# A convolution of width 3 with batch norm and SiLU: the first stage's loads, weights and jobs in another order

## The chip, the core and the metric

The kernel runs on one core of a Trainium2 chip. The metric is the device time of one execution in microseconds; lower is better. Before the change, three executions took 180.88, 180.94 and 181.14 us, a median of 180.94 us.

## The reference

The input `x` has 2 batches of 2048 positions with 1024 channels, all in bf16. Three 1024 x 1024 matrices `w[k]` are applied to the positions before, at and after each output position, the products are added, and a batch norm and SiLU follow:

```
xp = jnp.pad(x, ((0, 0), (P, P), (0, 0)))
y = sum(jnp.einsum('bsc,cd->bsd', xp[:, k:k + S, :], w[k]) for k in range(K))
inv_std = 1.0 / jnp.sqrt(var + 1e-5)
y = (y - mean) * (g * inv_std) + b
return _silu(y)
```

## The kernel before, in words

The kernel computes six neighbouring outputs from eight transformed inputs, with eight products instead of eighteen. The 2048 positions of a batch are cut into 342 groups of six. One input **transform** turns eight neighbouring positions of each group into eight numbers; it is a matmul of a window of 128 positions (the weights, `xw`) with a constant matrix `rm` of 8 x 21 columns (L241). One window gives 21 groups; 16 windows (`NF`) give 336 of them, and a **short** block of 48 rows (`xl`, L255) gives the last 6.

**Tiles.** `x` is loaded as 16 tiles of 512 KB, one for each batch `bi` and block `ct` of 128 channels; a tile has 128 partitions (positions in the window) of 16 windows x 128 channels. I call them tile (bi, ct). Six buffers hold them (`XBUFS`). The weights come by output block `dc` (eight of 128 channels), 768 KB each, in the order w0, w2, w1 (`W0, W2, W1`); for dc 0 the first two arrive in one transfer and w1 in a second.

**Jobs.** A tile's 16 windows are three jobs of 6, 6 and 4 transforms. `Jobs.do` writes a job into two of the eight PSUM banks (`BANKS`: A is banks 4 and 5, B is 6 and 7, C is 2 and 3, D is 0 and 1), and DVE or ACT or both copy the banks to `T_sb` in SBUF (casts of L264 on ACT and L266 on DVE). In the order of the first stage, written out by hand in `ORDER`, a token such as `Bda` is a job in B, its first bank copied by DVE and the second by ACT; `Ad` is a job in A whose two banks DVE copies in one instruction; `s2d` is the short block in bank 2. These three kinds are all of the transform work.

**Weights.** The products at points 0 and 7 use w0 and w2 as they are. The six others use sums: `even` adds two arrays on POOL (L134, or on DVE with L140 in the later stages), `transform_w` adds or subtracts w1 or its double (L147), so that `u0`, `u1`, `u2` each have a plus and a minus half. `FirstWeights` gives the order for dc 0, `prepare_second` that for dc 1, `prepare_w` that for the rest.

**The first unit.** `First` is the product of (dc 0, batch 0), spread through the first stage so that PE has something to do between jobs (L414). In `ORDER` a plain number stands for that many matmuls of points 0 and 7 (`ends`, 16 in all, into banks 2 and 3), `p` and a number for matmuls of the other points (`todo`, 48 in all, into banks 1, 0 and 2). `m2a` doubles w1 on ACT. `+` takes one entry of `later`, a list of DVE operations that combine the products (`combine`, L309). `kept` holds the points 0 and 7 after they left their banks (`COPIES` says by which engine a product is copied).

**Later stages.** 14 `Unit`s follow, each for one (dc, bi), on alternating halves of PSUM, and two `Half`s for the last; each unit has eight products of eight matmuls of 342 columns (L294).

**Queues.** Every engine runs its instructions in the order in which the program gives them. SP issues nearly all loads; ACT issues `rm` and `prm` (four rows of batch-norm parameters). `scales()` computes the batch norm's factors on POOL (L220 to L225), ahead of the first weights.

Of the kernel before, what the change touches and what calls it, by code (L numbers as in the profile page):

```python
# [8 lines left out]
ALU = mybir.AluOpType  # L9
# [5 lines left out]
R = 6  # L15
# [1 line left out]
WT = 21  # L17
XBUFS = 6
LROWS = 48
SROW = 66  # L20
NTILES = 342
NBP = 384


# [2 lines left out]

BANKS = {"A": 4, "B": 6, "C": 2, "D": 0}
ORDER = (
    "Bad Aad Da Cda Bda Ad Da Bda s2d Aad Dad Bad 2 Aa Dda 1 Bda Aad 1 Dad 1 Bda 1 Aa 1 Dda 1 Bda 1 Ada "  # L30
    "Dda Bad 1 m2a 2 Dd 2 Bda Aad Dda 2 Bad Aad p4 Ca p1 Bad p2 Aad Cda Ba p1 Ada p2 Ca p1 Bda p2 Aad p1 "
    "Ca p1 Bda p1 Aa p1 Cd p2 Bad p5 + Cad Ba p4 s4a Ca Bda Aa"
)

W0, W2, W1 = range(3)
COPIES = {0: "a", 7: "d", 1: "d", 3: "d", 2: "a", 5: "a"}

@with_exitstack
def kernel(
# [2 lines left out]
    x: bass.AP,  # L42
    xl: bass.AP,
    w: bass.AP,
    prm_in: bass.AP,
    rm_in: bass.AP,
    out: bass.AP,
):
    nc = tc.nc
    B, CT, _, NF, _ = x.shape  # L50
    DC = w.shape[0]
    NB = NTILES
    LAST = NB - NF * WT
    NT = NF * WT
    H = P

# [19 lines left out]
    T_sb = [tpool.tile([P, CT, NJ, NB], BF16, name=f"T_sb{bi}") for bi in range(B)]  # L76


    rm = consts.tile([P, NJ, WT], BF16, name="rm")
    nc.scalar.dma_start(out=rm, in_=rm_in)  # L80
    prm = consts.tile([P, 4, DC], BF16, name="prm")


    zero = consts.tile([P, 1], FP32, name="zero")
    nc.gpsimd.memset(zero, 0.0)
    for n in (384, 384, 216):
        nc.tensor.matmul(
            ps[:, 3, 0:n], lhsT=zero.broadcast_to([P, P]), rhs=zero.broadcast_to([P, n]), start=True, stop=True,
        )
    zeros = consts.tile([P, 64], FP32, name="zeros")  # L90
    nc.vector.memset(zeros, 0.0)
    dummy = consts.tile([P, 2], FP32, name="dummy")
    nc.vector.memset(dummy, 0.0)

# [4 lines left out]
    nc.vector.memset(small, 0.0)  # L99

    def load_small(bi):
        nc.sync.dma_start(out=small[bi * SROW:bi * SROW + LROWS], in_=xl[bi])

    def load_x(bi, ct):
        xt[bi, ct] = t = xpool.tile([P, NF, P], BF16, name="xw")
        nc.sync.dma_start(out=t, in_=x[bi, ct])  # L106

    def load_w(dc, taps=slice(0, 3)):
        if dc not in raw:
# [54 lines left out]
    class FirstWeights:  # L164
# [3 lines left out]
        def __init__(self, dc):  # L168
            w0, w2 = raw[dc][:, W0], raw[dc][:, W2]
            self.dc, self.src, self.made = dc, ((w2, 4.0), (w0, 4.0), (raw[dc][:, W1], 2.0)), {}  # L170
            elsewhere = [int(t[1]) for t in ORDER.split() if t[0] == "m"]
            self.steps = [(None, lambda: even(dc, 0, w0, w2))]
            self.steps += [(i, lambda i=i: self.multiple(i, nc.gpsimd)) for i in (0,) if i not in elsewhere]
            self.steps += [(0, lambda: even(dc, 1, self.made[0], w0))]
            self.steps += [(i, lambda i=i: self.multiple(i, nc.gpsimd)) for i in (1,) if i not in elsewhere]
            self.steps += [(1, lambda: even(dc, 2, self.made[1], w2))]
            self.steps += [(i, lambda i=i: self.multiple(i, nc.gpsimd)) for i in (2,) if i not in elsewhere]
            self.steps += [
                (2 if q else None, lambda q=q, i=i: transform_w(dc, q, (i,)))
                for q, i in ((0, 0), (1, 0), (0, 1), (1, 1), (2, 0), (2, 1))  # L180
            ]
            self.own = [i for i in range(3) if i not in elsewhere]

        def multiple(self, i, eng):
# [29 lines left out]
    beta = consts.tile([P, DC], FP32, name="beta")  # L214

    def scales():
        mhalf = consts.tile([P, DC], FP32, name="mhalf")
        nc.gpsimd.memset(mhalf, -0.5)
        sc = consts.tile([P, DC], FP32, name="sc")
        nc.gpsimd.tensor_scalar(sc, prm[:, 0, :], 1e-5, 1.0, op0=ALU.add, op1=ALU.mult)  # L220
        nc.gpsimd.tensor_tensor(sc, sc, mhalf, op=ALU.pow)
        nc.gpsimd.tensor_tensor(sc, prm[:, 1, :], sc, op=ALU.mult)
        nc.gpsimd.tensor_tensor(beta, prm[:, 2, :], sc, op=ALU.mult)
        nc.gpsimd.tensor_tensor(beta, prm[:, 3, :], beta, op=ALU.subtract)
        nc.gpsimd.tensor_scalar(scale, sc, 1.0 / 36.0, 0.0, op0=ALU.mult, op1=ALU.add)  # L225
# [3 lines left out]
    class Jobs:  # L229
# [20 lines left out]
        def do_short(self, bank, eng):  # L250
            bi = self.short.pop(0)
            src = ps[:, bank, 0:CT * NJ * LAST].rearrange("p (c j n) -> p c j n", j=NJ, n=LAST)
            rows, n = (slice(0, P), SROW // R) if bi else (slice(0, LROWS), 0)
            for c in range(CT):
                nc.tensor.matmul(  # L255
                    src[:, c], lhsT=small[rows, c * P:(c + 1) * P], rhs=rm[rows, :, n:n + LAST],
                    start=True, stop=True,
                )
            dst = T_sb[bi][:, :, :, NT:NB].rearrange("p c j n -> p (c j) n")
            self.out(dst, src.rearrange("p c j n -> p (c j) n"), eng)  # L260
# [127 lines left out]
    class First(Unit):  # L388
# [3 lines left out]
        def __init__(self, dc, bi):  # L392
            super().__init__(dc, bi, 0)
            self.sd = dpool.tile([P, 4, NB], FP32, name="sd")
            self.t = [
                consts.tile([P, 2, NB], FP32, name="f0"), ypool2.tile([P, 2, NB], FP32, name="t1"),
                consts.tile([P, 2, NB], FP32, name="f2"),
            ]
            self.kept = consts.tile([P, 2, NB], FP32, name="kept")
            self.ends = [(j, q, False, ct) for ct in range(CT) for j, q in ((0, 2), (NJ - 1, 3))]  # L400
            self.todo = [
                (j, q, add, ct) for j, q, add in (
                    (1, 1, False), (3, 0, False), (2, 1, True), (4, 0, True), (5, 2, False), (6, 2, True),
                ) for ct in range(CT)
            ]
            self.p, self.later = {}, []
# [20 lines left out]
        def behind(self, j, q):  # L427
            b0, b1 = self.bank[:2]
            sd = self.sd
            if j == 0 or j == NJ - 1:  # L430
                self.out_of(j, q, self.kept[:, j and 1])
            if j in (1, 3, 5):
                self.p[j] = cpool.tile([P, NB], FP32, name="pc")
                self.out_of(j, q, self.p[j], 4.0 if j == 3 else 1.0)
            if j == 1:
                self.combine(sd[:, 3], b1, 2.0, self.kept[:, 1])
            if j == 2:
                self.out_of(j, q, sd[:, 0])
                self.later += [
                    lambda: self.combine(sd[:, 1], b1, 1.0, self.kept[:, 0]),  # L440
                    lambda: self.combine(sd[:, 2], self.p[1], 2.0, b1, ALU.subtract),
                    lambda: self.combine(sd[:, 3], sd[:, 3], 1.0, b1, ALU.subtract),
                ]
            if j == 4:
                self.later.append(lambda: self.combine(b1, b0, -2.0, self.p[3]))
                for t, a, s in zip(self.t, (-0.0125, -0.05, -0.2), (sd[:, 1:3], sd[:, 0:3:2], sd[:, 0:4:3])):
                    self.later.append(lambda t=t, a=a, s=s: self.combine(t, self.low, a, s))
# [87 lines left out]

    nc.scalar.dma_start(out=prm, in_=prm_in)
    for ct in range(3):
        load_x(0, ct)  # L540
    load_small(0)
    load_w(0, slice(W0, W1))
    scales()
    nc.scalar.activation(dummy[:, 1:2], dummy[:, 0:1], ACT.Silu)
    for ct in range(3, CT):
        load_x(0, ct)
    load_w(0, slice(W1, W1 + 1))
    for ct in range(CT):
        load_x(1, ct)
    load_small(1)  # L550
    load_w(1)

# [3 lines left out]
    for token in ORDER.split():  # L558
        if token == "+":
            unit.later.pop(0)()  # L560
        elif token[0] == "m":
            first_w.multiple(int(token[1]), {"a": nc.scalar, "d": nc.vector}[token[2]])
            first_w.go()
        elif token[0] == "s":
            jobs.do_short(int(token[1]), token[2])
        elif token[0] in BANKS:
            jobs.do(BANKS[token[0]], token[1:])
        else:
            todo = unit.todo if token[0] == "p" else unit.ends
            for _ in range(int(token.lstrip("p"))):  # L570
                unit.do(todo)
    while unit.todo[0][0] == 4:
        unit.do(unit.todo)
    for f in unit.later:
        f()
# [32 lines left out]
    inner, outer = slice(2, R), slice(0, 2)  # L608
    h0 = Half(dc, bi, 4, 0)

    nc.tensor.matmul(ps[:, 5, 0:H], lhsT=zeros[:, 0:64].bitcast(BF16), rhs=T_sb[bi][:, 0, 0, 0:H], start=True, stop=True)  # L611
    h0.run(quiet, prev.rest(quiet, 5, 5))
    prev.store(nc.sync)
    h1 = Half(dc, bi, 0, 1)
# [21 lines left out]
def _laid_out(np, x, w, mean, var, g, b):  # L636
# [8 lines left out]
    xp[:, 1:S + 1] = x  # L645
    wins = np.stack([xp[:, f * step:f * step + P] for f in range(NF)], 2)
    wins = wins.reshape(B, P, NF, CT, P).transpose(0, 3, 1, 2, 4)
    rm = np.zeros((P, NJ, WT), np.float32)
    for n in range(WT):
        rm[R * n:R * n + NJ, :, n] = np.array(_POINTS, np.float32).T  # L650
    return (
        wins,
        xp[:, step * NF:step * NF + LROWS],
        w[[0, 2, 1]].reshape(K, CT, P, DC, P).transpose(3, 2, 0, 1, 4),
        np.stack([var, g, mean, b]).reshape(4, DC, P).transpose(2, 0, 1),
        rm.astype(x.dtype),
    )


# [28 lines left out]
```

## Time and profile before

| | |
|---|---|
| the profiled execution | 180.88 us |
| its span in the profile | 179.1 us |
| what lies around the span | 1.8 us |
| PE busy (matmuls) | 172.7 us, 96% |
| DVE, ACT, POOL busy | 147.6, 110.2, 139.7 us |
| granted TensorE clock | 1.00 throughout |
| read from HBM, written | 14.93 MB, 9.44 MB |

The span begins with the first instruction of the profiled execution and ends with the last; a time in the text is counted from its start. "x16" behind a line means sixteen instructions. A matmul's duration includes the drain of the array, so successive matmuls overlap: their starts are what shows PE's pace. The first 37 us load and transform the input; after that, PE runs the units.

### The profile page before, as it was taken

The numbers are of one execution on the slowest core, as the hardware profiler recorded it, in microseconds if no ns is written. First come the engines' busy times: TensorE is split into PE (matmuls) and PEld (weight loads), VectorE is DVE, ScalarE is ACT, GpSimd is POOL, SyncE is SP. The second block draws the span as 40 slices with busy tenths as digits, with TensorE's granted clock in tenths as the row PEclk, the third lists the DMA queues.
The fourth block names the chain that finished last, engine by engine and source line by source line (L and its number), as shares of the span: only waits on it lengthen the run. The fifth ranks groups of instructions, "written<-read, shape, count | busy, mean of one in ns | idle before, by whom it ended". The sixth has DMA issues, their size and how long they took to land.

```text
span 179.1 us, 3534 instructions
## 1 busy us (share of the span) xinstructions
PE 172.7 (96%) x1367; PEld 123.5 (69%) x1367; DVE 147.6 (82%) x211; ACT 110.2 (62%) x191; POOL 139.7 (78%) x77
## 2 busy tenths in 40 slices
PE   8879999999999999999999999999999999999991
PEld 4869888766666666666666666666666666668891
DVE  1779998897969999997878788898979987766691
ACT  3779999959374837374636654565356554563774
POOL 2599999999997799999999999999799959000000
PEclk9999999999999999999999999999999999999999
DMA  5999993450344031813082306330303030203033
GB/s 187 374 410 404 410 383 124 129 226 0 132 141 170 0 132 8 260 45 132 0 221 90 134 0 168 143 134 0 135 0 132 0 130 6 98 34 132 3 149 117
DMA packets 6912, 24.58 MB, mean 137 GB/s; under 512 B 1040, under 2 KB 1552, under 8 KB 6896
## 3 DMA queue, kind: packets, MB, share of 16 engines
q1 hardware_dynamic: 6464, 24.25, 36.8%
q8 instruction: 10, 0.16, 0.3%
q10 hardware_dynamic: 432, 0.12, 0.3%
q14 instruction: 6, 0.05, 0.1%
HBM read 14.93 MB, written 9.44 MB: 136 GB/s over the span
## 4 chain that ended last, share of the span: by engine, by line
PE 86%; DMA 8%; DVE 3%; ACT 1%; SPq 0%; issue 0%; DVEq 0%
PE ps L294 75%; DMA xw<-in_x_dram 8%; PE ps L241 6%; PE ps L414 4%; DVE ps L309 2%; DVE t L309 1%; ACT yh L313 1%; SPq L106 0%; PE ps L255 0%; DVEq L677 0%; DVE sd L309 0%; PE ps L611 0%; DVEq L309 0%
## 5 line engine op out<-in xcount | busy, mean ns | idle before, releaser
L294 PE MATMUL ps<-T_sb,u 128*128 128x342 bf16 (+2 forms) x768 | 109.4, 298 | 0.0
L294 PEld LDWEIGHTS <-u 128*128 128x128 bf16 x768 | 72.3, 97 | 32.6
L147 POOL TENSOR_TENSOR u<-e,w1x 128x1024 bf16<-128x1024 f32 x32 | 71.5, 2258 | 6.1 <-DVE e L140 6.0
L294 PE MATMUL ps<-T_sb,wch 128*128 128x342 bf16 (+2 forms) x256 | 39.5, 299 | 0.4 <-DVE ps L309 0.4
L309 DVE SCALAR_TENSOR_TENSOR t<-ps,sd 128x684 f32<-128x684 f32 (+2 forms) x49 | 37.6, 819 | 0.5
L313 ACT ACTIVATE yT<-ps,beta,scale 128x342 bf16<-128x342 f32 (+1 forms) x42 | 29.2, 727 | 12.6 <-PE ps L294 12.6
L147 POOL TENSOR_TENSOR u<-e,wch 128x1024 bf16<-128x1024 f32 x16 | 35.7, 2251 | 0.5
L294 PEld LDWEIGHTS <-wch 128*128 128x128 bf16 x256 | 24.2, 97 | 11.1 <-issue 0.5
L303 ACT COPY pc<-ps 128x342 f32<-128x342 f32 (+2 forms) x32 | 13.6, 425 | 27.9 <-PE ps L294 27.0
L266 DVE CAST T_sb<-ps 128x504 bf16<-128x504 f32 (+3 forms) x37 | 22.8, 664 | 6.8 <-PE ps L241 6.3
L264 ACT CAST T_sb<-ps 128x504 bf16<-128x504 f32 (+4 forms) x46 | 25.5, 640 | 3.7 <-PE ps L241 3.6
L309 DVE SCALAR_TENSOR_TENSOR ps<-ps,t 128x684 f32<-128x684 f32 (+2 forms) x32 | 26.5, 829 | 0.7
L309 DVE SCALAR_TENSOR_TENSOR ps<-ps,pc 128x342 f32<-128x342 f32 (+2 forms) x34 | 16.9, 498 | 11.5 <-PE ps L294 8.8
L241 PE MATMUL ps<-rm,xw 128*128 128x168 bf16 x256 | 23.2, 236 | 1.8 <-DMA xw<-in_x_dram 1.6
L241 PEld LDWEIGHTS <-xw 128*128 128x128 bf16 x256 | 19.7, 98 | 4.8 <-DMA xw<-in_x_dram 2.9
L140 DVE SCALAR_TENSOR_TENSOR e<-wch 128x1024 f32<-128x1024 bf16 x12 | 21.0, 1749 | 0.0
L134 POOL TENSOR_TENSOR e<-wch 128x1024 f32<-128x1024 bf16 x8 | 19.0, 2374 | 0.1
L313 ACT ACTIVATE yT<-t,beta,scale 128x684 bf16<-128x684 f32 x15 | 14.4, 958 | 0.0
L309 DVE SCALAR_TENSOR_TENSOR sd<-pc,ps 128x342 f32<-128x342 f32 (+2 forms) x17 | 8.2, 485 | 7.4 <-ACT sd L303 7.4
L309 DVE SCALAR_TENSOR_TENSOR t<-ps,t 128x684 f32<-128x684 f32 (+2 forms) x17 | 13.9, 817 | 0.0
L303 ACT COPY sd<-ps 128x342 f32<-128x342 f32 (+2 forms) x16 | 6.8, 428 | 10.6 <-PE ps L294 8.9
L305 ACT ACTIVATE pc<-ps 128x342 f32<-128x342 f32 (+2 forms) x16 | 7.0, 438 | 8.7 <-PE ps L294 6.0
(44 smaller groups left out, 68.2 us busy)
## 6 DMA issues: line engine op xcount, KB each, us to landing
out_dram<-yT SPq DMA_DIRECT2D x15, 576.0 KB, 2.8
xw<-in_x_dram SPq DMA_DIRECT2D x16, 512.0 KB, 7.2
wch<-in_w_dram SPq DMA_DIRECT2D x7, 768.0 KB, 5.5
wch<-in_w_dram SPq DMA_DIRECT2D x1, 512.0 KB, 6.5
wch<-in_w_dram SPq DMA_DIRECT2D x1, 256.0 KB, 8.5
out_dram<-yh SPq DMA_DIRECT2D x1, 256.0 KB, 2.1
xl<-in_xl_dram SPq DMA_DIRECT2D x2, 96.0 KB, 5.9
out_dram<-yh SPq DMA_DIRECT2D x1, 128.0 KB, 1.7
```

Source lines behind the costliest of these rows:

```text
L134: nc.gpsimd.tensor_tensor(sums[dc, q], a, b, op=ALU.add)
L140: nc.vector.scalar_tensor_tensor(out=e, in0=f, scalar=4.0, in1=h, op0=ALU.mult, op1=ALU.add)
L147: nc.gpsimd.tensor_tensor(wts[dc, q][:, i], sums[dc, q], o, op=(ALU.add, ALU.subtract)[i])
L241: nc.tensor.matmul(src[:, q // per, q % per], lhsT=xt[bi, ct][:, f + q], rhs=rm, start=True, stop=True)
L264: nc.scalar.copy(dst, src)
L266: nc.vector.tensor_copy(dst, src)
L294: nc.tensor.matmul(self.bank[q], lhsT=lhsT, rhs=T_sb[self.bi][:, ct, j, nsl], start=not add and ct == 0, stop=ct == CT - 1, skip_group_che ...
L303: nc.scalar.copy(dst, self.bank[q])
L305: nc.scalar.mul(dst, self.bank[q], by)
L309: nc.vector.scalar_tensor_tensor(out=out, in0=in0, scalar=scalar, in1=in1, op0=ALU.mult, op1=op1)
L313: nc.scalar.activation(self.yT[:, rows, self.y0:self.y0 + self.hi - self.lo], src, ACT.Silu, bias=beta[:, dc:dc + 1], scale=scale[:, dc:dc ...
L414: nc.tensor.matmul(self.bank[q], lhsT=lhsT, rhs=T_sb[self.bi][:, ct, j, :], start=not add and ct == 0, stop=ct == CT - 1, skip_group_check ...
```

## The change

- `rm` (8 x 21), a second matrix for the short blocks (8 x 6, zero below row 48) and the parameters come as one array `head` in one transfer on ACT, 496 bytes in each partition, in place of `rm` (336) and later `prm` (64).
- Tile (0, 0) is loaded by two transfers, the even rows and the odd rows. The second and all behind it are issued one place later on SP.
- w1 of dc 0 is loaded behind tile (0, 3) instead of behind tile (0, 7). `scales()` is written behind these loads.
- The short blocks' matmuls run over 128 rows; both use rows 0 to 47 of one buffer, so the second is loaded once the first has been used (in SP's order it stays where it was).
- `FirstWeights` finishes u0 before it starts u1, and u1 before u2.
- `ORDER` is a new list. The first unit's products come as 1, 2, 3, 4, 5, 6 instead of 1, 3, 2, 4, 5, 6. Point 7's copy moves from DVE to ACT.
- `kept` shares its memory with one of the unit's own tiles. Of the operations that make `sd[:, 3]`, two (each with one operand in PSUM) become one, whose two operands, `sd[:, 2]` and `kept[:, 1]`, both lie in SBUF.
- Two small constants go; the last of the warm-up matmuls on zeros has 192 columns instead of 216.

```
-    "Bad Aad Da Cda Bda Ad Da Bda s2d Aad Dad Bad 2 Aa Dda 1 Bda Aad 1 Dad 1 Bda 1 Aa 1 Dda 1 Bda 1 Ada "
-    "Dda Bad 1 m2a 2 Dd 2 Bda Aad Dda 2 Bad Aad p4 Ca p1 Bad p2 Aad Cda Ba p1 Ada p2 Ca p1 Bda p2 Aad p1 "
-    "Ca p1 Bda p1 Aa p1 Cd p2 Bad p5 + Cad Ba p4 s4a Ca Bda Aa"
+    "Dda Ada Cad Dad Ba Cad Ad Dd s3a Ba 4 Bda Ada Dd 2 m2a Bda Ada Dad 1 Bad 1 Aad p3 Bda p1 Ada p1 Bda "
+    "p1 Ada 2 Bda 1 Ada p1 Bda 2 Aad 2 p1 1 Bad Aa Cda p2 Bda p1 Ada Cda Bad Ada p5 + Ca + + p3 Bda p1 "
+    "Aad p1 Cad p1 Bad Aa p2 Cad Ba p3 Ada Cda p1 Bda Ada p1 Cda Bad Aa p1 s3a"
-COPIES = {0: "a", 7: "d", 1: "d", 3: "d", 2: "a", 5: "a"}
+COPIES = {0: "a", 7: "a", 1: "d", 3: "d", 2: "a", 5: "a"}
...
     def load_x(bi, ct):
         xt[bi, ct] = t = xpool.tile([P, NF, P], BF16, name="xw")
-        nc.sync.dma_start(out=t, in_=x[bi, ct])
+
+        step = 1 if bi or ct else 2
+        for q in range(step):
+            nc.sync.dma_start(out=t[q::step], in_=x[bi * CT + ct, q::step])
...
+            self.steps = [(None, lambda: even(dc, 0, w0, w2))] + weights(0)
+            self.steps += multiple(0) + [(0, lambda: even(dc, 1, self.made[0], w0))] + multiple(2) + weights(1)
+            self.steps += multiple(1) + [(1, lambda: even(dc, 2, self.made[1], w2))] + weights(2)
...
                 (j, q, add, ct) for j, q, add in (
-                    (1, 1, False), (3, 0, False), (2, 1, True), (4, 0, True), (5, 2, False), (6, 2, True),
+                    (1, 1, False), (2, 1, True), (3, 0, False), (4, 0, True), (5, 2, False), (6, 2, True),
                 ) for ct in range(CT)
...
-            if j == 1:
-                self.combine(sd[:, 3], b1, 2.0, self.kept[:, 1])
             if j == 2:
                 self.out_of(j, q, sd[:, 0])
                 self.later += [
                     lambda: self.combine(sd[:, 1], b1, 1.0, self.kept[:, 0]),
                     lambda: self.combine(sd[:, 2], self.p[1], 2.0, b1, ALU.subtract),
-                    lambda: self.combine(sd[:, 3], sd[:, 3], 1.0, b1, ALU.subtract),
+                    lambda: self.combine(sd[:, 3], sd[:, 2], 1.0, self.kept[:, 1]),
                 ]
...
     load_small(0)
     load_w(0, slice(W0, W1))
+    load_x(0, 3)
+    load_w(0, slice(W1, W1 + 1))
     scales()
     nc.scalar.activation(dummy[:, 1:2], dummy[:, 0:1], ACT.Silu)
-    for ct in range(3, CT):
+    for ct in range(4, CT):
         load_x(0, ct)
-    load_w(0, slice(W1, W1 + 1))
```

More of the change, by code (lines that the diff above doesn't have):

```diff
@@ L19 @@
 LROWS = 48
-SROW = 66
 NTILES = 342
+LAST = 6
 NBP = 384
@@ L44 @@
     w: bass.AP,
-    prm_in: bass.AP,
-    rm_in: bass.AP,
+    head: bass.AP,
     out: bass.AP,
@@ L49 @@
     nc = tc.nc
-    B, CT, _, NF, _ = x.shape
-    DC = w.shape[0]
+    NF = x.shape[2]
+    B, DC = out.shape[:2]
+    CT = w.shape[3]
     NB = NTILES
-    LAST = NB - NF * WT
     NT = NF * WT
@@ L76 @@
     T_sb = [tpool.tile([P, CT, NJ, NB], BF16, name=f"T_sb{bi}") for bi in range(B)]
-    rm = consts.tile([P, NJ, WT], BF16, name="rm")
-    nc.scalar.dma_start(out=rm, in_=rm_in)
-    prm = consts.tile([P, 4, DC], BF16, name="prm")
+    ends = (0, NJ * WT, NJ * (WT + LAST))
+    first = consts.tile([P, head.shape[1]], BF16, name="head")
+    nc.scalar.dma_start(out=first, in_=head)
+    rm = first[:, :ends[1]].rearrange("p (j n) -> p j n", j=NJ)
+    rm_short = first[:, ends[1]:ends[2]].rearrange("p (j n) -> p j n", j=NJ)
+    prm = first[:, ends[2]:].rearrange("p (i d) -> p i d", i=4)
     zero = consts.tile([P, 1], FP32, name="zero")
     nc.gpsimd.memset(zero, 0.0)
-    for n in (384, 384, 216):
+    for n in (384, 384, 192):
         nc.tensor.matmul(
@@ L89 @@
         )
-    zeros = consts.tile([P, 64], FP32, name="zeros")
-    nc.vector.memset(zeros, 0.0)
     dummy = consts.tile([P, 2], FP32, name="dummy")
@@ L101, in load_small @@
     def load_small(bi):
-        nc.sync.dma_start(out=small[bi * SROW:bi * SROW + LROWS], in_=xl[bi])
+        nc.sync.dma_start(out=small[:LROWS], in_=xl[bi])
     def load_x(bi, ct):
         xt[bi, ct] = t = xpool.tile([P, NF, P], BF16, name="xw")
-        nc.sync.dma_start(out=t, in_=x[bi, ct])
+        step = 1 if bi or ct else 2
+        for q in range(step):
+            nc.sync.dma_start(out=t[q::step], in_=x[bi * CT + ct, q::step])
     def load_w(dc, taps=slice(0, 3)):
@@ L171, in __init__, with multiple, weights @@
             elsewhere = [int(t[1]) for t in ORDER.split() if t[0] == "m"]
[L172 to L181, printed above, removed]
+            def multiple(i):
+                return [(i, lambda: self.multiple(i, nc.gpsimd))] if i not in elsewhere else []
+            def weights(q):
+                return [(2 if q else None, lambda i=i: transform_w(dc, q, (i,))) for i in (0, 1)]
+            self.steps = [(None, lambda: even(dc, 0, w0, w2))] + weights(0)
+            self.steps += multiple(0) + [(0, lambda: even(dc, 1, self.made[0], w0))] + multiple(2) + weights(1)
+            self.steps += multiple(1) + [(1, lambda: even(dc, 2, self.made[1], w2))] + weights(2)
             self.own = [i for i in range(3) if i not in elsewhere]
@@ L216, in scales @@
     def scales():
-        mhalf = consts.tile([P, DC], FP32, name="mhalf")
-        nc.gpsimd.memset(mhalf, -0.5)
+        nc.gpsimd.memset(scale, -0.5)
         sc = consts.tile([P, DC], FP32, name="sc")
         nc.gpsimd.tensor_scalar(sc, prm[:, 0, :], 1e-5, 1.0, op0=ALU.add, op1=ALU.mult)
-        nc.gpsimd.tensor_tensor(sc, sc, mhalf, op=ALU.pow)
+        nc.gpsimd.tensor_tensor(sc, sc, scale, op=ALU.pow)
         nc.gpsimd.tensor_tensor(sc, prm[:, 1, :], sc, op=ALU.mult)
@@ L252, in do_short @@
             src = ps[:, bank, 0:CT * NJ * LAST].rearrange("p (c j n) -> p c j n", j=NJ, n=LAST)
-            rows, n = (slice(0, P), SROW // R) if bi else (slice(0, LROWS), 0)
             for c in range(CT):
                 nc.tensor.matmul(
-                    src[:, c], lhsT=small[rows, c * P:(c + 1) * P], rhs=rm[rows, :, n:n + LAST],
-                    start=True, stop=True,
+                    src[:, c], lhsT=small[:, c * P:(c + 1) * P], rhs=rm_short, start=True, stop=True,
                 )
@@ L398, in __init__ @@
             ]
-            self.kept = consts.tile([P, 2, NB], FP32, name="kept")
+            self.kept = self.t[2]
             self.ends = [(j, q, False, ct) for ct in range(CT) for j, q in ((0, 2), (NJ - 1, 3))]
@@ L534, in store @@
             queue.dma_start(out=self.to[:, rows], in_=self.yT[:, rows])
-    nc.scalar.dma_start(out=prm, in_=prm_in)
     for ct in range(3):
@@ L542 @@
     load_w(0, slice(W0, W1))
+    load_x(0, 3)
+    load_w(0, slice(W1, W1 + 1))
     scales()
     nc.scalar.activation(dummy[:, 1:2], dummy[:, 0:1], ACT.Silu)
-    for ct in range(3, CT):
+    for ct in range(4, CT):
         load_x(0, ct)
-    load_w(0, slice(W1, W1 + 1))
     for ct in range(CT):
         load_x(1, ct)
-    load_small(1)
-    load_w(1)
     first_w = FirstWeights(0)
@@ L565 @@
             jobs.do_short(int(token[1]), token[2])
+            if jobs.short:
+                load_small(1)
+                load_w(1)
         elif token[0] in BANKS:
@@ L571 @@
                 unit.do(todo)
-    while unit.todo[0][0] == 4:
+    while unit.todo[0][0] != 5:
         unit.do(unit.todo)
@@ L609 @@
     h0 = Half(dc, bi, 4, 0)
-    nc.tensor.matmul(ps[:, 5, 0:H], lhsT=zeros[:, 0:64].bitcast(BF16), rhs=T_sb[bi][:, 0, 0, 0:H], start=True, stop=True)
+    nc.tensor.matmul(ps[:, 5, 0:H], lhsT=zero.bitcast(BF16)[:, 0:1].broadcast_to([P, P]), rhs=T_sb[bi][:, 0, 0, 0:H], start=True, stop=True)
     h0.run(quiet, prev.rest(quiet, 5, 5))
@@ L647, in _laid_out @@
     wins = wins.reshape(B, P, NF, CT, P).transpose(0, 3, 1, 2, 4)
-    rm = np.zeros((P, NJ, WT), np.float32)
+    rm, short = np.zeros((P, NJ, WT), np.float32), np.zeros((P, NJ, LAST), np.float32)
     for n in range(WT):
         rm[R * n:R * n + NJ, :, n] = np.array(_POINTS, np.float32).T
+    short[:LROWS] = rm[:LROWS, :, :LAST]
+    prm = np.stack([var, g, mean, b]).reshape(4, DC, P).transpose(2, 0, 1)
+    wins = wins.reshape(B * CT, P, NF, P)
     return (
@@ L654, in _laid_out @@
         w[[0, 2, 1]].reshape(K, CT, P, DC, P).transpose(3, 2, 0, 1, 4),
-        np.stack([var, g, mean, b]).reshape(4, DC, P).transpose(2, 0, 1),
-        rm.astype(x.dtype),
+        np.concatenate([a.reshape(P, -1).astype(x.dtype) for a in (rm, short, prm)], 1),
     )
@@ L669 @@
     given = {k: _np.asarray(v) for k, v in inputs.items()}
-    for name, a in zip(("x", "xl", "w", "prm", "rm"), _laid_out(_np, **given)):
+    for name, a in zip(("x", "xl", "w", "head"), _laid_out(_np, **given)):
         a = _np.ascontiguousarray(a)
```

## The prediction

> **What bounds the kernel now.** I read the chain that ended last first, in order of time:
>
> ```profile
> 1.63 5.85 DMA xw<-in_x_dram
> ...
> 9.31 9.27 DMA xw<-in_x_dram
> ...
> 36.84 126.54 PE ps L294 x872
> ```
>
> From 36.84 us on, PE runs units without a break (126.54/872 = 0.145 us for each matmul). What the change touches lies before that, where the chain waits for input twice. The timeline of PE shows what the waits cost:
>
> ```profile
> 7.52 1.04 PE L241 MATMUL ps<-rm,xw 128*128 128x168 bf16 x12 [0.28 <-DMA xw<-in_x_dram]
> 8.50 0.39 PE L255 MATMUL ps<-rm,xl 48*128 48x48 bf16 x8
> 8.81 0.46 PE L241 MATMUL ps<-rm,xw 128*128 128x168 bf16 x4
> 10.38 1.04 PE L241 MATMUL ps<-rm,xw 128*128 128x168 bf16 x12 [1.10 <-DMA xw<-in_x_dram]
> ...
> 18.63 1.33 PE L241 MATMUL ps<-rm,xw 128*128 128x168 bf16 x16 [0.18 <-DMA xw<-in_x_dram]
> ```
>
> By starts, a transform takes 0.073 us and a product 0.145. Between the first transform (4.71 us) and 18.63, PE did 128 transforms (9.31 us), 8 short ones (0.21) and 14 products of the ends (2.03): 11.55 of 13.92, so 2.37 us were lost; later only 0.14. No change of order can win more than these 2.5 us. The stages show what else is full:
>
> ```profile
> 6.00:8.00 2.00, 1.72 (x25) 1.51 (x23) 2.00 (x5) 1.83 (x4) 1.76 (x2) 1.00 1.03 338
> 8.00:10.00 2.00, 1.28 (x20) 0.89 (x17) 2.00 (x4) 1.82 (x3) 1.63 (x6) 1.00 1.04 412
> 10.00:18.60 8.60, 8.06 (x94) 7.09 (x94) 7.45 (x14) 7.63 (x15) 8.28 (x6) 1.00 1.03 406
> 18.60:24.00 5.40, 5.37 (x64) 4.90 (x65) 5.15 (x10) 5.09 (x11) 5.40 (x3) 1.00 1.03 410
> 24.00:30.00 6.00, 6.00 (x69) 5.20 (x67) 5.32 (x11) 5.68 (x10) 6.00 (x4) 1.00 0.74 267
> ```
>
> The columns after the length are PE, weight loads, DVE, ACT, POOL, clock, DMA share, GB/s. The loads are at their ceiling (406 GB/s: one tile in 1.29 us) until 28 us, and DVE, ACT and POOL have a few tenths of a microsecond to spare in each stage. A DVE operation that is late has nowhere to hide.
>
> **The early loads.** Tile (0, 3) is there at 10.38; the pace puts w0/w2 at 9.1. With w1 (256 KB, 0.65 us) ahead of it, tile (0, 4) comes at about 12.26 instead of 11.6. From tile (0, 7) on the order in the stream is the old one. One transfer fewer (`prm`) and one more (half of tile (0, 0)) leave SP's eight in flight as they were. `head` gates the first transform as `rm` does; 496 bytes instead of 336 in a transfer that lands beside a 512 KB tile I cost at nothing, because tile (0, 1) paces PE next and tile (0, 2) leaves 0.45 us idle before 7.52; past that cover it costs what it is late.
>
> Two half tiles: no row shows one. The nearest is the short block's load, 48 partitions: the stretch 6 to 8 us moves 338 GB/s against 407 (402 before it, 412 behind), (407 - 338) x 2 us = 138 KB or 0.34 us lost. Bounds: 0.3 us gained (the stream starts sooner, for it moves only 0.3 of a tile by 2.4 us), or 2 x 0.34 lost. Every second row spans all partitions where the 48 rows span the lower ones, so I take a value near nothing: 0.1 us late.
>
> **PE until 19 us, walked job by job.** The four ends before tile (0, 3) fill 0.58 of the idle 1.27 us before 10.38 (they wait for w0 at 9.1 and the short block's copy at about 9.3). Tile (0, 3) and two ends last until 11.88; tile (0, 4) is there at 12.26, a new gap of 0.4. From then on tiles are there when PE asks. What limits is A and B, two jobs in flight: a bank is free about 1.1 to 1.3 us after its job began (DVE's cast of 504 columns 0.68 us, ACT's 0.60, behind the job itself 0.43), which gives stalls of some 0.2 us. u0 plus is made by 13.4 (see POOL), ahead of `p3` at 14.6. So PE begins tile (1, 0) at 19.13 with 13 ends and 7 products behind it: six products more than before at 18.63. 6 x 0.145 - 0.50 = 0.37 us ahead; with the 0.14 of later stalls that before had, 0.51 us ahead if the rest ran without a stall.
>
> **POOL.** Same adds (2.13 us), in another order: `scales()` ends sooner, even 0 starts when w0 is there (9.1 instead of 9.28), but five adds instead of three have to wait for the one directly before (0.08 us instead of an overlap of 0.05). The end of u2 stays at 30.6. Even 0 9.1-11.2, u0 to 15.5, multiple and even 1 to 18.8, u1 to 23.1, multiple to 24.1, even 2 24.2-26.3, u2 to 30.6. Each is ready before the product that needs it (p 17 at 24.8, p 25 at 29.5, point 5 at 33). What POOL's pace leaves for an earlier PE shows behind:
>
> ```profile
> 45.56 4.23 POOL L147 TENSOR_TENSOR u<-e,w1x 128x1024 bf16<-128x1024 f32 x2
> ...
> 48.29 1.33 PE L294 MATMUL ps<-T_sb,u 128*128 128x342 bf16 x8
> ```
>
> The first of the two adds ends at 47.69 and PE uses it at 48.29: PE can be at most 0.6 us earlier than now, whatever `ORDER` does.
>
> **The new DVE operation.** The third `+` computes `sd[:, 3]` from two operands in SBUF. In the before kernel every L309 of this stage has an operand in PSUM and takes 0.50 us beside POOL. The one DVE operation with two SBUF operands is L140 of the later stages:
>
> ```profile
> 65.53 2.65 DVE L140 SCALAR_TENSOR_TENSOR e<-wch 128x1024 f32<-128x1024 bf16 x1
> ...
> 62.87 4.23 POOL L147 TENSOR_TENSOR u<-e,w1x 128x1024 bf16<-128x1024 f32 x2 [1.23 <-DVE e L140]
> 67.04 3.12 POOL L134 TENSOR_TENSOR e<-wch 128x1024 f32<-128x1024 bf16 x1
> ```
>
> It starts at 65.53 inside an add of POOL, ends 1.08 us after that add (67.10) and lasts 2.65 us instead of the 1.21 of its shortest; the add behind lasts 3.12 instead of 2.13. Each waits for the other. By the nearest row in size (L309, 342 columns) the new operation costs 0.50 and replaces two, a gain; by the nearest in kind it waits for the running add. I take the kind.
>
> The Trainium skill states this as a rule (SBUF — State Buffer, Who interferes with whom): a DVE instruction with two SBUF inputs and a GpSimd instruction that reads SBUF exclude each other for a whole instruction. By that rule the sum is the +0.32 below; by the L309 row it would be -0.51.
>
> How long it waits: DVE is busy without a gap from 19.6 (casts 0.61 from start to start, copies and combines 0.42). The fifth product of `p5` ends the group at 24.35; DVE does the casts of tile (1, 2) until 24.8, then the first `+` to 25.2, the second to 25.6, and asks for the third at 25.65. Even 2 runs until 26.3, a wait of 0.65 us; the operation ends at 26.8. Queued behind it on DVE: the first bank of B (job `Bda` of tile (1, 3), whose matmuls are done at 25.66), then the cast of `Aad` and all that follow. PE meets it at the next `Bad` (tile (1, 4)), due at 26.82: bank 6 is free at 27.5 instead of 26.8, a stall of 0.68 us. DVE then stays behind, and `p3` waits for the copy of point 3 (29.5 against 29.38), 0.15 more. Without the wait the same walk has no stall there. Bounds: the request is good to some 0.4 us, so the stall is 0.3 to 1.1; if DVE asks after 26.3, it meets the next add and waits up to 2.1. POOL loses 0.45 us once: u2 of dc 1 comes at 48.1, when a PE that is late anyway needs it at 48.6.
>
> **The rest at nothing.** Moving point 7's copy to ACT (0.5 us) is hidden: C is used again 0.7 us later. Fewer combines after the loop (0.5 us of DVE) lie beside PE's points 4 and 5. 24 columns less of warm-up end before the tile lands. The tail is not touched.
>
> **Sum.** 180.88 us (span 179.1 and 1.8 around it) - 0.51 + 0.68 + 0.15 + 0.1 = 181.3. The profiled execution stands 0.06 below the median of the three runs, 180.94. About 0.2%, 0.36 us, is what a measurement can tell from no change.
>
> **The rivals.** (a) The blocked operation costs nothing, because DVE asks in one of POOL's short pauses or the exclusion does not hold for this form. For it: 0.50 us in all rows of L309; against: L140 waited each time that an add was running. Then PE is 0.51 - 0.1 ahead, within POOL's 0.6: 180.45. (b) The halves of tile (0, 0) lose the stream 0.34 to 0.68 us, as the 48 rows did; tiles (0, 2) to (0, 4) and w0, hence PE and POOL, are late by that: 181.6 to 181.9. For it: the 338 GB/s; against: all partitions are spanned. (c) DVE asks after 26.3 and waits for u2's whole add, 2.1 us: PE's stall grows by 1.4, 182.7. It decides if DVE is 0.7 us later than walked. (d) DVE and ACT have more slack than I gave them and the stalls stay under 0.5 us: 180.8, the change does nothing.
>
> **How the numbers follow.** The forecast, 181.3, has 0.45; its own range by the wait is 180.9 to 181.8, of which two thirds lie over 181.24. (a) has 0.25, nearly all faster; (b) 0.14, slower; (c) 0.06, slower; (d) 0.10, within. Slower: 0.30 + 0.14 + 0.06 = 0.50. Within: 0.15 + 0.10 + 0.02 of (a) = 0.27. Faster: 0.23. The range takes in (a) and most of (b), and leaves out (c): 180.35 to 182.1.
>
> **What would show it.** Right: one L309 on DVE with `sd` and `kept` as operands, near 25.7 us, of over 0.9 us, and beside it an add of POOL of some 2.6 us; behind it a stall of PE at a job in bank 6; the gap before tile (0, 3) halved, a new one of 0.4 before tile (0, 4); the chain of PE without a break reached about 0.3 us later than at present. Wrong: that operation lasts 0.5 us; or PE's first transform of tile (0, 2) starts well after 7.5 us; or unit (1, 0) stalls at 48 us for u2.

## The result and the profile after

The changed kernel takes 183.45 us (median of 182.77, 183.28, 183.62 and 186.28), the kernel before 180.92 beside it: a ratio of 1.0125, with an interval of 1.0094 to 1.0156. An execution over 1.5% above the fastest of its kernel (186.28 here, 187.73 of a_cols below) counts in a median but not in a ratio. The kernel is slower, as forecast, but by 2.5 us (2.3 by the ratio) and not by 0.4; 183.45 lies outside the range of 180.35 to 182.1. The profiled execution took 183.28 us and its span is 181.4.

The chain that ended last shows that everything is decided by 39 us. Behind it stands the same long piece of PE as before (126.54 us there):

```profile
5.41 8.61 DMA xw<-in_x_dram
...
27.70 0.93 DVE sd L309
28.63 0.61 DVE T_sb L266
29.28 0.89 PE ps L243 x10
...
39.23 126.55 PE ps L294 x872
```

The piece begins 2.39 us later (39.23 against 36.84). In both kernels the time from unit (dc 0, batch 1)'s first matmul to the end of the span is 144.7 us (34.36 to 179.05 before, 36.74 to 181.45 after). So I read only what comes ahead of that matmul. The chain names two things there: a transfer of `x`, and a new DVE operation. The timeline of PE shows the first:

```profile
4.58 1.43 PE L243 MATMUL ps<-head,xw 128*128 128x168 bf16 x16
7.66 1.33 PE L243 MATMUL ps<-head,xw 128*128 128x168 bf16 x16 [1.65 <-DMA xw<-in_x_dram]
9.21 1.04 PE L243 MATMUL ps<-head,xw 128*128 128x168 bf16 x12 [0.22 <-DMA xw<-in_x_dram]
...
12.12 1.33 PE L243 MATMUL ps<-head,xw 128*128 128x168 bf16 x16 [0.35 <-DMA xw<-in_x_dram]
```

Tile (0, 0) is used at 4.58, as early as before (4.71). Then PE is idle for 1.65 us, because tile (0, 1) is there at 7.6 instead of 5.9, and tile (0, 2) at 9.2 instead of 7.5. That is the sign of being wrong that I had named: tile (0, 2) well after 7.5 us. The delay is never made up: tile (1, 0) begins at 20.82 where my walk had 19.13. By stages (the columns as in the prediction, the last two DMA share and GB/s), first one stage of the kernel before, then the kernel after:

```profile
4.00:6.00 2.00, 1.81 (x20) 1.37 (x19) 0.61 (x2) 0.83 (x2) 0.00 (x0) 1.00 1.03 402
```

```profile
4.00:6.00 2.00, 1.85 (x18) 1.25 (x16) 0.89 (x2) 0.67 (x2) 1.43 (x5) 1.00 0.84 231
6.00:8.00 2.00, 0.35 (x6) 0.35 (x6) 0.80 (x2) 0.73 (x2) 0.00 (x0) 1.00 0.95 333
8.00:10.00 2.00, 1.78 (x25) 1.57 (x23) 1.23 (x3) 1.85 (x3) 0.00 (x0) 1.00 1.03 364
10.00:18.60 8.60, 7.65 (x92) 6.25 (x90) 8.24 (x13) 6.61 (x14) 7.49 (x5) 1.00 1.03 406
```

The stream moved 231 GB/s from 4 to 6 us (before 402) and 364 from 8 to 10 (before 412). (402 + 338 + 412) - (231 + 333 + 364) = 224 GB/s over 2 us each is 448 KB; at 406 GB/s that is 1.1 us. From 10 us on the stream moves the same 406 GB/s in both kernels, so what was lost stays lost. A tile can be used only when its last share has landed, and the shares of the sixteen DMA engines (the trace has a semaphore update for each) are spread further: those of tile (0, 3) land from 10.62 to 12.07 us, before from 9.97 to 10.34. So the first share is 0.65 us later, and the last, which PE waits for, 1.73.

The second thing is the DVE operation with two SBUF operands. Timelines of DVE, of POOL, and of PE:

```profile
26.73 0.51 DVE L309 SCALAR_TENSOR_TENSOR sd<-ps,f 128x342 f32<-128x342 f32 x1 [0.27 <-ACT sd L424]
27.16 0.50 DVE L309 SCALAR_TENSOR_TENSOR sd<-pc,ps 128x342 f32<-128x342 f32 x1
27.70 0.93 DVE L309 SCALAR_TENSOR_TENSOR sd<-sd,f 128x342 f32<-128x342 f32 x1
```

```profile
26.13 2.12 POOL L137 TENSOR_TENSOR e<-w1x,wch 128x1024 f32<-128x1024 bf16 x1
28.33 4.37 POOL L150 TENSOR_TENSOR u<-e,w1x 128x1024 bf16<-128x1024 f32 x2
```

```profile
28.36 0.31 PE L415 MATMUL ps<-T_sb,u 128*128 128x342 bf16 x1
29.28 0.89 PE L243 MATMUL ps<-head,xw 128*128 128x168 bf16 x10 [0.61 <-DVE T_sb L266]
```

It starts at 27.70, while an add of POOL runs (26.13 to 28.26), ends 0.37 us after that add and lasts 0.93 us instead of the 0.50 of its neighbours. PE then stalls at a job in bank 6: by starts 28.36 + 0.15 to 29.28, 0.77 us.

### The profile page after: what moved, and what is told of

Its sections match the earlier page's. It is cut to its first block, busy times and chain, and to the rows that moved or that the text cites. A ratio compares the mean times of both kernels' runs of the same rounds, so it can differ in the third digit from the quotient of the medians.

```text
span 181.4 us, 3537 instructions
## 1 busy us (share of the span) xinstructions
PE 173.3 (96%) x1367; PEld 123.2 (68%) x1367; DVE 149.6 (82%) x212; ACT 109.6 (60%) x193; POOL 139.9 (77%) x77
## 4 chain that ended last, share of the span: by engine, by line
PE 84%; DMA 5%; DVE 4%; ACT 3%; SPq 2%; issue 1%; DVEq 0%
PE ps L294 74%; PE ps L243 6%; DMA xw<-in_x_dram 5%; PE ps L415 4%; ACT T_sb L264 2%; DVE ps L309 2%; SPq L109 1%; DVE sd L309 1%; DVE t L309 1%; SPq L114 1%; ACT yh L313 1%; DVE T_sb L266 0%; ACT sd L424 0%; SPq L102 0%; DVEq L679 0%
## 5 line engine op out<-in xcount | busy, mean ns | idle before, releaser
L150 POOL TENSOR_TENSOR u<-e,w1x 128x1024 bf16<-128x1024 f32 x32 | 70.6, 2228 | 6.5 <-DVE e L143 4.9
L266 DVE CAST T_sb<-ps 128x504 bf16<-128x504 f32 (+3 forms) x41 | 24.6, 659 | 7.0 <-PE ps L243 6.7
L264 ACT CAST T_sb<-ps 128x504 bf16<-128x504 f32 (+4 forms) x47 | 24.6, 600 | 7.2 <-PE ps L243 6.4
L243 PE MATMUL ps<-head,xw 128*128 128x168 bf16 x256 | 23.2, 237 | 3.3 <-DMA xw<-in_x_dram 2.5
L137 POOL TENSOR_TENSOR e<-wch 128x1024 f32<-128x1024 bf16 x8 | 19.9, 2491 | 5.3 <-DMA wch<-in_w_dram 5.3
L143 DVE SCALAR_TENSOR_TENSOR e<-wch 128x1024 f32<-128x1024 bf16 x12 | 21.8, 1812 | 0.0
```

The source lines that it names most:

```text
L137: nc.gpsimd.tensor_tensor(sums[dc, q], a, b, op=ALU.add)
L143: nc.vector.scalar_tensor_tensor(out=e, in0=f, scalar=4.0, in1=h, op0=ALU.mult, op1=ALU.add)
L150: nc.gpsimd.tensor_tensor(wts[dc, q][:, i], sums[dc, q], o, op=(ALU.add, ALU.subtract)[i])
L243: nc.tensor.matmul(src[:, q // per, q % per], lhsT=xt[bi, ct][:, f + q], rhs=rm, start=True, stop=True)
L264: nc.scalar.copy(dst, src)
L266: nc.vector.tensor_copy(dst, src)
```

## Experiments

All times are medians; a ratio is to runs of the kernel before on the same chip (medians of 180.92 to 181.03 us). It is not the quotient of the medians, and differs from it by up to 0.0015 where runs spread. There are two suspects, the split of tile (0, 0) and the DVE operation, and as rivals the warm-up that is 24 columns shorter, the merged head and the new place of w1. The names: "whole" is the kernel after with tile (0, 0) in one transfer, "psum" has `sd[:, 3]` made as before.

**Tile (0, 0) in one transfer** (a_whole), on the kernel after:

```
-        step = 1 if bi or ct else 2
+        step = 1
```

> The changed kernel with tile (0, 0) in one transfer again. Theory H (the two half tiles stagger the engines of the loads, and the stream of all later tiles is late by 1.1 to 1.8 us): PE's first transform of tile (0, 1) comes at about 5.9 us instead of 7.66, tile (0, 4) is asked for at 12.3 instead of 14.06, and the time falls by 1.4 to 1.8 us, to 181.7 to 182.0; the stall behind the DVE operation on sd and kept (0.77 us) stays. Rival R (the merged first transfer or w1's new place delays the stream): tile (0, 1) still comes after 7 us and the time stays within 0.3 us of 183.4.

181.83 us, ratio 1.0039 (1.0023 to 1.0055): 1.6 us of the loss is this one line. Tile (0, 1) has landed at 5.63 instead of 7.61 and begins at 6.52 instead of 7.66 (PE's own pace sets the 6.52, see the end), tile (1, 0) at 19.47 instead of 20.82. The DVE operation is as it was (26.34, 0.95 us), with the same stall of PE, 0.78 us. So the two losses are separate. In the three kernels that have the operation (after, this one and a_cols below) it lasts 0.93, 0.95 and 0.92 us; POOL's add ends 0.56, 0.57 and 0.55 us after its start, and each time 0.37 us are left: it waits for the add.

**`sd[:, 3]` in two operations that read PSUM** (a_psum), on the kernel after; in `ORDER` the last product of point 7 changes places with the last of point 1, since the first operation needs both:

```
-                self.out_of(j, q, self.p[j], 4.0 if j == 3 else 1.0)
+                self.out_of(j, q, self.p[j], 4.0 if j == 3 else 1.0); j == 1 and self.combine(sd[:, 3], b1, 2.0, self.kept[:, 1])
...
-                    lambda: self.combine(sd[:, 3], sd[:, 2], 1.0, self.kept[:, 1]),
+                    lambda: self.combine(sd[:, 3], sd[:, 3], 1.0, b1, ALU.subtract),
```

> The changed kernel with sd[:, 3] formed as before, in two DVE operations with one operand in PSUM each (one product of point 1 and the last one of point 7 change places for it). Theory P (the operation with two SBUF operands waits for POOL's running add and holds PE up): no L309 of that stage lasts over 0.6 us, PE's stall of 0.77 us at 28.4 goes, the time falls by 0.6 to 0.8 us to about 182.7. Rival: DVE is simply full there, PE's stall moves to a neighbouring job and the time falls by less than 0.3.

182.98 us, ratio 1.0100 (1.0072 to 1.0127), 0.47 less than the kernel after and less than the 0.6 to 0.8 that I expected. The two intervals overlap, so this pair of times alone does not show the gain; the traces do. Its timeline of DVE has the operation at its ordinary length:

```profile
28.19 0.50 DVE L309 SCALAR_TENSOR_TENSOR sd<-sd,ps 128x342 f32<-128x342 f32 x1
```

PE's largest stall in that stretch falls from 0.77 to 0.23 us. From the first matmul of tile (1, 0) to that of unit (dc 0, batch 1), the three kernels with one operation take 15.92 to 15.95 us, and the four with two (this one and the three below made from it) 15.37 to 15.38: 0.55 us.

**Both** (a_whole_psum):

> Both: tile (0, 0) in one transfer and sd[:, 3] in two operations. If H and P add up: 183.4 - 1.6 - 0.7 = 181.1; the walk of the prediction without its two losses gives 180.4. If PE is then held by u2 of dc 1 at 48 us, not below 180.3.

181.32 us, ratio 1.0008 (0.9991 to 1.0026): the effects add up (183.45 - 1.62 - 0.47 = 181.36). But this is no faster than the kernel before, although my walk without the two losses said 180.4. That is a second error, followed further down.

**The split alone** (b_split), the kernel before with tile (0, 0) in even and odd rows:

```
-        nc.sync.dma_start(out=t, in_=x[bi, ct])
+        for q in range(1 if bi or ct else 2): nc.sync.dma_start(out=t[q::1 if bi or ct else 2], in_=x[bi, ct, q::1 if bi or ct else 2])
```

> The kernel before with only one thing changed: tile (0, 0) in two transfers, even and odd rows. Theory H: tile (0, 1) late by 1.5 to 1.8 us, time 182.3 to 182.7. Rival R: no change, 180.9 within 0.3.

182.79 us, ratio 1.0101 (1.0069 to 1.0134): 1.83 us. Nothing else of the change is in this kernel. Its stages:

```profile
4.00:6.00 2.00, 0.81 (x5) 0.33 (x4) 0.00 (x0) 0.00 (x0) 1.84 (x3) 1.00 0.92 231
6.00:8.00 2.00, 2.00 (x16) 1.77 (x13) 1.10 (x2) 1.18 (x2) 0.77 (x4) 1.00 0.93 352
8.00:10.00 2.00, 2.00 (x16) 1.99 (x16) 1.38 (x3) 1.39 (x3) 0.00 (x0) 1.00 1.03 342
```

Again 231 GB/s from 4 to 6 us. PE shows another thing: 16 matmuls fill 2 us, so a transform takes about twice its time (0.14 us from start to start and not 0.07). Did the loads or PE's pace cost the time? The timeline of PE decides it:

```profile
5.70 5.54 PE L241 MATMUL ps<-rm,xw 128*128 128x168 bf16 x44 [1.19 <-DMA xw<-in_x_dram]
...
12.52 1.04 PE L241 MATMUL ps<-rm,xw 128*128 128x168 bf16 x12 [0.56 <-DMA xw<-in_x_dram]
```

Even at half pace PE is through with tile (0, 2) before tile (0, 3) is there, and waits 0.56 us for it, until 12.52 (before: 10.38). The loads cost the time. Here the second half itself is late: it has landed at 5.57 us, after the 4.46 of the whole tile before.

**Two halves of neighbouring rows** (b_halves): rows 0 to 63, then 64 to 127, on the kernel before.

> The kernel before with tile (0, 0) in two transfers of 64 rows each, rows 0 to 63 and 64 to 127, instead of even and odd rows. Theory S (a second transfer of 64 rows in front is what holds up the descriptors of tile (0, 1), whichever rows it has): tile (0, 1) lands after 7 us, spread over 1.5 to 2 us from the first engine to the last, 182.5 to 183. Rival E (alternate rows make two engines of the loads meet): contiguous halves lose less than 0.5 us, 181.0 to 181.4.

182.71 us, ratio 1.0083 (1.0062 to 1.0104), tile (0, 3) at 12.55. The two halves land at 4.56 and 5.83. Alternate rows are not the cause.

**The warm-up** (b_192: the kernel before with 192 columns; awp_216: "whole" and "psum" with 216):

```
-    for n in (384, 384, 216):
+    for n in (384, 384, 192):
```

> The kernel before with one thing changed: the last two warm-up matmuls have 192 columns instead of 216. Theory C (the shorter warm-up lets the clock rise a window later in many executions; in the profiles so far the first transforms start 0.07 us apart from 4.9 us on in two kernels and 0.14 us apart until 6.3, 6.9, 10.1 and 10.2 in four): median over 181.3, with a wide spread up to 182.3. Rival I (what decides is that PE idles when the first tiles come late, not these 24 columns): 180.95, as before.

> The changed kernel with tile (0, 0) in one transfer and sd[:, 3] in two operations, and with the warm-up of 216 columns again. Theory C: transforms at full pace from 4.9 us, median down from 181.3 to 180.5 to 180.8. Rival I: 181.3, as without the 24 columns.

180.99 us, ratio 1.0000 (0.9991 to 1.0009), and 181.80, ratio 1.0042 (1.0024 to 1.0060) where the same kernel with 192 columns has 1.0008. The shorter warm-up costs nothing, and the longer one mends nothing. With 216 the runs also spread further (181.04 to 182.63 instead of 180.89 to 181.61), which is not explained: the two profiled executions are alike, 181.48 and 181.61.

**The merged head** (b_head: `rm` and `prm` as one array in one transfer, on the kernel before) and **w1 behind tile (0, 3)** (b_w1), then both (b_head_w1):

```
-    load_w(0, slice(W0, W1))
+    load_w(0, slice(W0, W1)); load_x(0, 3); load_w(0, slice(W1, W1 + 1))
...
-    for ct in range(3, CT):
+    for ct in range(4, CT):
...
-    load_w(0, slice(W1, W1 + 1))
```

> The kernel before with one thing changed: rm and prm come in one transfer. Theory M (with the second small transfer gone, the engines of the loads drift apart on tiles (0, 1) and (0, 2), as in the two kernels with tile (0, 0) in one transfer, where tile (0, 2) came 0.3 to 0.7 us later than before): 181.2 to 181.6. Rival: nothing, 180.95; then w1's new place or chance makes the drift.

> The kernel before with one thing changed: w1 of dc 0 is loaded behind tile (0, 3). By the pace of the loads tile (0, 4) comes 0.65 us later; the old ORDER has two ends to cover 0.3 of it: 181.2 to 181.4. If the early w1 also lets the engines drift, PE's wait for tile (0, 2) grows as well: 181.5 or more. Rival: the evictions hide it, 180.95.

> The kernel before with rm and prm in one transfer and w1 behind tile (0, 3): each alone took 180.76 and 181.13. Theory Q (with both, one more load stands in SP's queue before 5.6 us, and the engines drift apart on tile (0, 2), as in the three kernels made from the changed one with tile (0, 0) whole): tile (0, 2) lands at 7.7 to 8.2 us, its engines over 1 us apart, tile (0, 4) is asked for after 12.7, 181.3 to 181.7. Rival (the drift comes from something else in the changed kernel): tile (0, 2) at 7.5, the two effects add up to 180.95.

b_head: 180.76 us, ratio 0.9987 (0.9978 to 0.9996), 0.2 us faster than the kernel before and the fastest kernel of the study. b_w1: 181.13, ratio 1.0010 (1.0000 to 1.0019); tile (0, 4) begins at 12.44 (before 11.84, forecast 12.26) and PE does not make it up with the old `ORDER`. Both: 180.91, ratio 0.9993 (0.9983 to 1.0002), the sum of the two. In b_head_w1 tile (0, 2) has landed at 7.50 (before 7.47; 7.72 in b_w1), so together these two changes of the queue do not hold up the stream, and theory Q, as it was put, falls.

**`prm` in a transfer of its own** (awp_two), on "whole" and "psum":

> The changed kernel with tile (0, 0) whole, sd[:, 3] in two operations, and prm again in a transfer of its own behind the matrices. Theory Q: no drift, tile (0, 2) at 7.5 to 7.8, tile (0, 4) asked for at 12.4, PE at tile (1, 0) at 19.3; the evictions' stalls of 0.7 us behind it stay, 181.0 to 181.2. Rival: drift as before, 181.3 to 181.8.

181.24 us, ratio 1.0004 (0.9993 to 1.0015), and all runs within 0.3 us. Tile (0, 2) has landed at 7.65 (8.20 in a_whole_psum). Here the new order is seen without the split, without the blocked operation and without a late stream: tile (1, 0) begins at 19.21, where the walk said 19.13. The first matmul of unit (dc 0, batch 1) nevertheless stands at 34.58, against 34.36 before. Between them, PE's starts show stalls of 0.15, 0.08, 0.10, 0.23 and 0.13 us, 0.69 in all, each at a job or product that waits until DVE has emptied a bank.

**Two transfers with all 128 rows each** (b_cols on the kernel before, a_cols on the kernel after): windows 0 to 7, then 8 to 15.

```
-        nc.sync.dma_start(out=t, in_=x[bi, ct])
+        n = NF if bi or ct else NF // 2
+        for q in range(0, NF, n):
+            nc.sync.dma_start(out=t[:, q:q + n], in_=x[bi, ct, :, q:q + n])
```

> The kernel before, with tile (0, 0) in two transfers that each span all 128 rows: windows 0 to 7, then windows 8 to 15. Theory S (a transfer of 64 rows in front of the stream is what costs): no such transfer is left, so SP issues in 0.43 us each, tile (0, 1) has landed at 5.9 us, the first transforms of tiles (0, 1) to (0, 3) start at 5.9, 7.5 and 10.4, and the time is 180.9 to 181.2. Theory N (any second transfer in front of the stream costs, whatever its rows, because each issue of SP then comes one place later): SP's issues take 0.56 us or more, tile (0, 2) starts near 8.2 to 9.2 and the time is 182.5 to 183.

> The kernel after, with tile (0, 0) in two transfers by windows (0 to 7, 8 to 15) in place of even and odd rows. Theory S: as with the tile in one transfer, tile (1, 0) starts near 19.5 and the time is 181.6 to 182.1; the DVE operation beside POOL keeps its 0.93 us and PE's stall of 0.77. Theory N: as the kernel after, tile (1, 0) near 20.8, 183.0 to 183.6.

b_cols: 181.98 us, ratio 1.0046 (1.0029 to 1.0062), 0.95 us; a_cols: 183.46, ratio 1.0128 (1.0111 to 1.0145), the same as with alternate rows. So my theory S (only a transfer of 64 rows costs) falls: on the kernel after, full rows cost just as much. Theory N (any second transfer in front costs) holds in sign, with b_cols below the 182.5 that it asked for, and its reason falls too: it wanted SP's issues to take 0.56 us, and in a_cols they take 0.37 to 0.43. The timeline of PE in a_cols:

```profile
4.23 2.32 PE L243 MATMUL ps<-head,xw 128*128 128x168 bf16 x16
8.17 2.41 PE L243 MATMUL ps<-head,xw 128*128 128x168 bf16 x28 [1.62 <-DMA xw<-in_x_dram]
...
12.38 1.34 PE L243 MATMUL ps<-head,xw 128*128 128x168 bf16 x16 [0.29 <-DMA xw<-in_x_dram]
```

The profiled execution of b_cols took 183.71 us, 1.7 above the median, so I read only its start. What came behind is a fall of the clock: PE's transforms are 0.14 us apart from about 11.4 to 14.8 us, and the granted clock of that stage is 0.80:

```profile
10.00:18.60 8.60, 7.46 (x72) 6.72 (x70) 5.90 (x11) 6.29 (x13) 8.25 (x5) 0.80 1.03 406
```

3.4 us at half pace are 1.7 us of work lost, about as much as this execution is above the median. One column carries the comparison of all these kernels, when PE begins tile (0, 3), which PE waits for in each of them but awp_two (there the product ahead of it ends as the tile comes). Tile (0, 1) is no such measure: in a_whole and awp_two it had landed at 5.63 and 5.95, and PE came to it later by its own pace.

| kernel | tile (0, 1) | tile (0, 3) | median us |
|---|---|---|---|
| before | 5.91 | 10.38 | 180.95 |
| b_cols | 6.49 | 11.29 | 181.98 |
| b_split | 8.02 | 12.52 | 182.79 |
| b_halves | 8.16 | 12.55 | 182.71 |
| awp_two | 6.71 | 10.50 | 181.24 |
| a_whole | 6.52 | 10.76 | 181.83 |
| after | 7.66 | 12.12 | 183.45 |
| a_cols | 8.17 | 12.38 | 183.46 |

From before to b_cols, b_split and b_halves the tile is later by 0.91, 2.14 and 2.17 us and the time longer than in the runs beside it by 0.95, 1.83 and 1.76; from a_whole to after and a_cols, 1.36 and 1.62 against 1.62 and 1.63. The time follows the stream, as far as one profiled execution of each kernel can show it.

## Why the prediction was wrong

**The step that failed: "Two half tiles … I take a value near nothing: 0.1 us late."** It measured 1.62 us on the kernel after and 1.83 on the kernel before, outside even my bounds (0.3 gained to 0.68 lost). I had no row of two transfers in place of one, took the short block as the nearest, asked how many partitions a transfer spans, and did not ask what the stream behind it does in its first microseconds. In the profile of after the loss comes behind the halves: they have landed at 3.71 and 4.45 us (the whole tile before: 4.46), but of tile (0, 1) the sixteen shares land between 5.60 and 7.61, where before all landed between 5.47 and 5.86. In b_split and b_halves the second half is late too. The engines are not merely idle: from 4 to 6 us their busy share falls from 1.03 to 0.84 (b_split: 0.92), much less than the rate, 402 to 231 GB/s in both. The rest is that packets take longer: by the packet records of the traces, those of 4096 bytes took 0.24 us on average (b_split: 0.26, the longest 1.47) and before 0.16. Rival (b) had the right place and sign, and well under half of the size.

**"0.51 us ahead if the rest ran without a stall"** was the second miss, of 0.77 us. The walk to 19 us was good (19.13 against 19.21 in awp_two, 0.08 late; even in the kernel after, PE idles 0.35 us before tile (0, 3), 1.10 in the kernel before, and 0.33 before tile (0, 4), where I had 0.4). Behind it I did not walk job by job: there the new order has 0.69 us of stalls for banks, where I counted none; the 0.14 of the old order were already in my 0.51. 0.51 - 0.08 - 0.69 = -0.26: the new order is no faster, and in the trace 0.22 us later (34.58 against 34.36). By its runs awp_two is not told from the kernel before (0.9993 to 1.0015).

**The new DVE operation was right in kind and place, and near in size.** Forecast: over 0.9 us, behind a running add, then a stall of 0.68 at bank 6. Measured: 0.93 us, behind a running add, then a stall of 0.77 at bank 6; all 2 us later than forecast, since the stream is late. Undone, it gives 0.47 to 0.51 us back by the medians and 0.55 by the traces, less than the stall, since other stalls for banks come in its place. Only the neighbouring add was less drawn out than I said: the first of POOL's two took 2.28 us, not 2.6. The rule of the Trainium skill (SBUF — State Buffer, Who interferes with whom) agrees with the trace: 0.93 and 0.95 us with two SBUF operands, 0.50 with one in PSUM. Rival (a), no wait, is out, and so is (c), a wait of a whole add.

**The terms at nothing held:** the shorter warm-up (0.0 us), `head` (0.2 us gained instead of lost). The weights were ready in time: unit (dc 1, batch 0) runs without a gap. The first of the two adds of u2 ends at 49.99 us, and PE uses it at 50.68, right behind the eight matmuls before (by starts, 49.52 + 8 x 0.145).

```profile
47.86 4.22 POOL L150 TENSOR_TENSOR u<-e,w1x 128x1024 bf16<-128x1024 f32 x2
```

```profile
49.52 1.32 PE L294 MATMUL ps<-T_sb,wch 128*128 128x342 bf16 x8
50.68 1.33 PE L294 MATMUL ps<-T_sb,u 128*128 128x342 bf16 x8
```

**The sum with the measured terms.** Tile (1, 0) at 20.82 instead of 19.13 is +1.69, of which 0.1 was in the forecast; 1.35 go with the split, and 0.34 are still there in a_whole (19.47). The stalls behind it are 0.77 + 0.13 + 0.17 + 0.16 = 1.23 instead of 0.68 + 0.15, +0.40. 181.3 + 1.59 + 0.40 = 183.29, and the profiled execution took 183.28. Since both kernels take the same 144.7 us from unit (dc 0, batch 1) on, such a sum has to close; it says where the time went, not why.

**What stays open.** Why packets take longer and some DMA engines fall behind after a second transfer in front is not settled. Alternate rows, the number of rows, SP's longer issue and the shorter warm-up are each excluded as the sole cause; that half the rows in each transfer cost 1.8 us and all rows 0.95 on the kernel before, but the same on the kernel after, is not explained. Nor is it that a_whole, whose tile (0, 0) is whole, still has a slow stretch (342 GB/s from 4 to 6 us) that awp_two (411) does not have; each figure is of one execution, and the runs of a_whole spread over 1.15 us, those of awp_two over 0.30.

## What to carry to other kernels

When the input stream is the bound, measure before cutting the large transfer at its head: cutting it cost 0.95 to 1.83 us here, though in the kernel after the first piece was there 0.75 us sooner (3.71 against 4.46). See when the last DMA engine delivers the *next* tiles, not when the first piece lands. An operation whose operands move from PSUM to SBUF may have to wait for the rest of POOL's running instruction, as here for 0.55 to 0.57 us. An order written out by hand has to be walked to its end, since what is won in the first half can be lost in the second to waits for banks.

## What the runs showed of the hardware that I had not expected

- A split of the first transfer changes SP's issue: in the kernels with two transfers of 64 rows, each of the first three issues takes 0.56 to 0.59 us, in all others 0.37 to 0.43. The chain that ended last, in the profile of after:

```profile
0.72 0.56 SPq L109
1.34 0.57 SPq L109
1.96 0.59 SPq L109
2.58 0.43 SPq L109
```

- The small transfer on ACT comes sooner in those kernels: `head` had landed at 2.3 to 2.6 us in the kernel after, `rm` at 4.3 to 4.7 in the kernel before, together with tile (0, 0) (4.1 to 4.5).
- PE's transforms run at half pace (0.14 us from start to start instead of 0.07) until a moment that differs between executions: 4.8 us in the kernels before and after, 5.4 in b_192, 6.2 to 6.9 in six others, 10.1 to 10.3 in a_psum, b_split and b_halves, whose first transform came late (5.4 to 6.0). The clock column shows 1.00 in these early stages; the pace is seen only in the starts. The later fall in b_cols does show in it, as 0.80. The Trainium skill (TensorE: Matmul & The Clock Gate, What's actually happening) says that the array runs at half clock until a window of about 3.4 us was busy, and that the window's place differs from run to run; the traces agree that the moment varies. It cost little where tile (0, 3) was waited for anyway, as in b_split.
